# Retention and a gated projection in one Trainium2 kernel: sums asked for with the scores, batch 1's transposes in other banks and sooner, the first stage reordered

## The chip, the cores and the metric

The kernel runs on one core of one Trainium2 chip. The metric is the device time of one execution in microseconds (us). The core's engines are named here as in the profile: PE (TensorE, matrix multiplication), DVE (VectorE), ACT (ScalarE), POOL (GpSimd) and SP (SyncE, which issues the DMAs).

## The reference

Eight batches of eight heads, 576 positions and 64 channels per head. Retention is attention with a decay by distance in place of a softmax; its output is the input of a feed-forward part with a SiLU gate.

```python
scale = 1.0 / np.sqrt(D_)
scores = scale * np.matmul(q, k.transpose(0, 1, 3, 2))
gamma = 1.0 - 2.0 ** (-5.0 - np.arange(H, dtype=np.float32))
rel = pos[:, None] - pos[None, :]
Dmat = np.where(rel >= 0, gamma[:, None, None] ** rel[None, :, :], 0.0)
ret = scores * Dmat[None, :, :, :]
attn = np.matmul(ret, v)                       # (8, 8, 576, 64)
x = attn.transpose(0, 2, 1, 3).reshape(4608, 512)
h = x @ w_in                                   # 512 -> 2048
g = h * (1.0 / (1.0 + np.exp(-beta * h)))
out = g @ w_out                                # 2048 -> 512
```

## The kernel before

**Retention in chunks.** The decay is split into a factor for each query row (`gq`) and one for each key row (`gv`, put on v). A batch's first 512 positions are four chunks of 128; the last 64 positions of all batches are gathered into four tail chunks that form a ninth block. Within a chunk the kernel takes scores, masks them on DVE (`R`) and multiplies by v. Earlier chunks come in through a state, the sum of k-transposed times v over the chunks so far, which is multiplied by q (`a_cross`, `crosses4`). The output lands already transposed in `xT`, the input of the feed-forward part.

**Batches 0 and 1.** These two go through `spans`: two spans of 256 rows, each span in two interleaved halves `r`. `pre_q`, `pre_k` and `pre_v` scale and cast q, k and v to bf16 (`qs`, `kn`, `vn`); `t_q` and `t_k` transpose on PE into a PSUM tile `T` that is copied to `qT` and `kT`; `a_sc` makes scores (one `R` for each row half of the array; a last argument of 0 or 1 masks one of the two at a time); `states` and `state_out` build the state and copy it to `sbd`; `a_O` and `a_cross` make the output `O`; `a_x` copies it to `xT`. `second(i)` does the last three for the chunks `i` and `i + 1` of batch 1. Later batches are transposed by DMA (`x_q`, `x_k`).

**Feed-forward.** `up`, `ups` and `up_spans` multiply `w_in` by `xT`, one tile of 128 of the 2,048 features (`fo`) at a time, into a PSUM tile `ph`; ACT applies SiLU. Blocks 0 to 2 then go through `down`, a plain projection with `w_out` (four row tiles `ms`, in steps of four `fo`). From block 3 (`SB`) on, the down projection is done with seven products in place of eight (`seven_a`, `seven_mm`, `seven_out`), and an odd `fo` takes a second step on DVE (L776), which multiplies by a ratio.

**Folds.** From block 2 on, the states of four eighths at a time are made beside the scores, in two PSUM banks, one of `mm` and one of `st` (`state_banks`). `fold` adds them one after the other to running sums on DVE (L585) and casts the sums to bf16. The banks are free when their sums are taken. One of the sums is held in the tile `warm`, whose zeros served the warm-up before.

**PSUM.** Eight banks: `mm` has three, `O` and `sc` two each, `st` one.

**Order.** Everything is written out by hand. The first stage (L928 to L986) is a list of calls, in the order in which each engine takes its work. Between its calls stand warm-up matmuls on zeros (`warm_up`), f32, of 256 or 128 columns; a f32 matmul is two pairs of a weight load and a matmul in the trace. Everything after is `merged`: `fill` holds PE's dense steps (up and down), numbered from 0, and `streams` hold the other steps, each with the number of the fill step ahead of which it is issued. `d0` is the number of batch 0's first down step, `u1` = `d0` + 16 that of batch 1's first up step, and the steps `d0` + 12 to `d0` + 15 are the last row tile of batch 0's down projection. From block 3 on, `t0` is the step ahead of which a block's scores are issued, and `queued` hands out the rest of that work (folds, casts, masks) at the listed steps.

Of the kernel before, what the change touches and what calls it, by code (L numbers as in the profile page):

```python
# [19 lines left out]
def kernel(  # L20
# [10 lines left out]
    nc = tc.nc  # L31
# [230 lines left out]
    for g in range(NP):  # L262
        load_w_in(g)

    def warm_up(n, cols=256, tag="mm"):
        ph = psum.tile([P, MB], F32, name="ph", tag=tag, bufs=dict(mm=3, st=1)[tag])
        for _ in range(n):
            nc.tensor.matmul(ph[:, :cols], warm[:, :P], warm[:, :cols], start=True, stop=True,
                             skip_group_check=True)

    def betas():
# [30 lines left out]
    def gains(g, c):  # L302
        return g[:, c, :].unsqueeze(2).to_broadcast([P, H, D])
# [73 lines left out]
            live.update({b * CB + 2 * u + x: {} for x in range(2)})  # L377
        copy(spans[b, u]["kn"][:, r], span_tiles[b, u, 0][:, :, r])  # L378

    def pre_v(b, u, r, multiply=nc.gpsimd.tensor_tensor):  # L380

        vn = spans[b, u]["vn"][r] = sb.tile([P, H, D], BF16, name="vn", tag="vn", bufs=7)
        multiply(vn[:], span_tiles[b, u, 1][:, :, r], gains(gv, 2 * u + r), ALU.mult)
# [23 lines left out]

    def t_k(b, u, r):
        late_span = b and u
        T = psum.tile([P, HP, P], BF16, name="T", tag="sc" if late_span else "mm" if b + u + r == 0 else "O",  # L410
                      bufs=3 if b + u + r == 0 else 2)
        for p in range(HP):
            nc.tensor.transpose(T[:, p, :], heads(spans[b, u]["kn"][:, r], p), ident[:])  # L413
        (nc.vector.tensor_copy if late_span or b == 0 and u != r else nc.scalar.copy)(spans[b, u]["kT"][:, r], T[:])
# [346 lines left out]
    def up(m, fo, c0=0, cn=CB):  # L761
        if m not in gts:
            gts[m] = sb.tile([P, FO, CB, P], BF16, name="gT", tag="gT", bufs=1)
        w = slice(c0 * PC, (c0 + cn) * PC)
        ph = psum.tile([P, CB, P], F32, name="ph", tag="mm", bufs=3)
        ph = ph.rearrange("f i s -> f (i s)")[:, :cn * P].rearrange("f (i s) -> f i s", i=CB)
        ns = 2 if m == SB and fo in halved else 1
        for ko in range(KO):
            for n in range(ns):
                cs = slice(n * CB // ns, (n + 1) * CB // ns)  # L770
                nc.tensor.matmul(ph[:, cs], w_in_sb[:, ko, fo * P:(fo + 1) * P], xts[m][:, ko, cs, w],  # L771
                                 start=(ko == 0 and n == 0), stop=(ko == KO - 1), skip_group_check=ns > 1)
        if m >= SB and fo % 2:
            h = scratch[0][:, fo // 2 % 4].rearrange("f (i s) -> f i s", i=CB)
            nc.scalar.activation(h, ph, ACT.Silu, scale=beta_sb[:, fo:fo + 1])  # L775
            nc.vector.tensor_scalar(gts[m][:, fo], h, ratio[:, fo // 2:fo // 2 + 1], None, ALU.mult)  # L776
            return
        nc.scalar.activation(gts[m][:, fo, :, w], ph, ACT.Silu, scale=beta_sb[:, fo:fo + 1])  # L778
# [146 lines left out]

    warm_up(1)  # L928
    betas()
    betas_safe()  # L930
    warm_up(3)
    for n in range(2):
        pre_q(0, n)
    pre_k(0, 0, 1, nc.vector.tensor_copy)
# [3 lines left out]
    t_k(0, 0, 0)  # L938
    for n in range(2, 4):
        pre_q(0, n)  # L940
    warm_up(1, 128)
    a_sc(0, 0, 0, 0)
    warm_up(1, 128)
    t_q(0, 1, slice(0, 2), nc.scalar.copy)
    t_q(0, 1, slice(2, CB), nc.vector.tensor_copy)
    a_sc(0, 0, 0, 1)
    pre_k(0, 1, 0)
    pre_k(0, 1, 1, nc.scalar.copy)
    warm_up(1, 128)
    t_k(0, 1, 0)  # L950
    t_k(0, 1, 1)
    pre_v(0, 0, 0)
    a_sc(0, 0, 1, 0)
    pre_v(0, 0, 1, nc.vector.tensor_tensor)
    a_sc(0, 0, 1, 1)
    a_sc(0, 1, 0)
    warm_up(2, 128, "st")
    states(0, 0)
    a_sc(0, 1, 1)
    states(0, 1)  # L960
    state_out(0, 0)
    state_out(0, 1)
    for r in range(2):
        pre_v(0, 1, r)
    for c in range(2):
        new_O(c)
    a_O(0, 0, 0)
    a_O(0, 0, 1, last=False)
    a_x(0)
    a_cross(1, False)  # L970
# [52 lines left out]
    def second(i):  # L1023
# [3 lines left out]
        if i > CB:  # L1027
# [12 lines left out]
               [(d0 + 7, F(pre_q, 1, n)) for n in range(4)] + [(d0 + 12.5, F(pre_q, XB, n)) for n in range(4)] + [(d0 + 11.6, F(t_q, 1, 0)), (d0 + 12.6, F(t_q, 1, 1))],  # L1040
               [(d0 + 8, F(pre_k, 1, 0, r)) for r in range(2)] + [(d0 + 9, F(pre_v, 1, 0, r)) for r in range(2)] +
               [(d0 + 12.6, F(t_k, 1, 0, 0)), (d0 + 12.6, F(t_k, 1, 0, 1)), (d0 + 14, F(a_sc, 1, 0, 0)), (d0 + 14, F(a_sc, 1, 0, 1)),
                (d0 + 14, F(states, 1, 0)), (d0 + 14, F(state_out, 1, 0)), (d0 + 14, F(state_out, 1, 1)), (d0 + 15.9, F(second, 4))],
# [71 lines left out]
    for n in range(1, B):  # L1115

        take = [i for i in todo if seq[i][0] == n + 1 or n == B - 1]
        todo = todo[len(take):]
        b, t = n + 1, base[n]
        t0 = t + lead.get(n, 0)  # L1120
        if n == 1:
            at = [t + 17, base[b] - 8.3]
        elif n < SB:
            at = [t + 3, t + 18]
        else:
            at = [t0 - 13, t0 + 2] if n < B - 1 else [t0 - 9.5, t0 - 2.5]
        for i, x in zip(take, at, strict=True):
            streams.append(pair_prep(i, x))
        if n == 1:
            streams.append([(d0 + 6.1, F(mask, late, [1, CB], [CB, PC // 2])),  # L1130
                            (d0 + 6.2, F(mask, tri, [1, TL]))])
            streams.append([(at[0], F(group1, b, (0,))), (at[1], F(group1, b, (1,))), (at[1] + 4.1, F(both4, b))])
        elif n < SB:
            streams.append([(t + 16, F(first_states, b))] * (b == XB + 1) +
                           [(t + 19, F(group1, b, (0, 1))), (t + 25.9, F(both4, b))])
        elif n == B - 1:
            outs = []
            streams.append([(t0, F(tail_scores, take[0])), (t + 13, F(both_tails, take[0], outs))] +
                           queued([t + 16.3, t + 17.6, t + 20.5, t + 22.5], outs))
# [41 lines left out]
```

## Time and profile before

| | |
|---|---|
| time, median of 3 runs | 290.85 us (290.37 to 290.99) |
| profiled execution: time, span | 290.9 us, 289.2 us |
| PE busy | 281.4 us, 97% of the span |
| DVE, ACT, POOL busy | 185.3, 169.7, 134.7 us |
| granted PE clock | 1.00 |
| data moved by DMA | 54.05 MB, 187 GB/s on average |

The span runs from the first to the last instruction; the time of the execution has 1.7 us more. All times inside the span are counted from its start. PE's matmuls overlap, and their ends are modelled, so the time that PE loses at a wait is read from one start to the next.

### The profile page before, as it was taken

How to read it: one execution, taken by the hardware profiler on the slowest of the kernel's cores; microseconds unless marked ns; L12 is line 12 of the kernel's file. 1: busy time of each engine (PE TensorE's matmuls, PEld its weight loads, DVE VectorE, ACT ScalarE, POOL GpSimd, SP SyncE). 2: the span in 40 equal slices, each digit the busy share in tenths (PEclk: the TensorE clock that was granted, in tenths of full speed). 3: DMA queues.
4: the chain of work that ended last, by engine and by line, in shares of the span. 5: the costliest groups of instructions: out<-in, count | busy, mean ns of one | idle time of the engine just before them, and what ended most of it. 6: DMA issues, size and time to landing. Idle time of an engine off the chain costs nothing.

```text
span 289.2 us, 8713 instructions
## 1 busy us (share of the span) xinstructions
PE 281.4 (97%) x3643; PEld 178.1 (62%) x3643; DVE 185.3 (64%) x343; ACT 169.7 (59%) x295; POOL 134.7 (47%) x258
## 2 busy tenths in 40 slices
PE   6899999999999999999999999999999999999995
PEld 4564446874454445568854884578557845884584
DVE  5983545714798287289759865995598455642673
ACT  4367727586968892775358615771576156827730
POOL 6366019933993874197587466634089300000000
PEclk9999999999999999999999999999999999999999
DMA  6999999977999999989899999990689330002004
GB/s 216 305 363 385 382 307 294 175 161 195 194 174 277 248 156 207 291 204 168 189 260 246 169 258 247 186 148 0 211 178 163 74 147 3 2 37 108 2 4 141
DMA packets 120567, 54.05 MB, mean 187 GB/s; under 512 B 93888, under 2 KB 113360, under 8 KB 120528
## 3 DMA queue, kind: packets, MB, share of 16 engines
q1 hardware_dynamic: 120496, 53.49, 79.6%
q8 instruction: 28, 0.46, 0.7%
q14 instruction: 11, 0.09, 0.1%
q10 hardware_dynamic: 32, 0.01, 0.0%
HBM read 36.71 MB, written 9.44 MB: 160 GB/s over the span
## 4 chain that ended last, share of the span: by engine, by line
PE 93%; DMA 3%; DVE 1%; issue 1%; SPq 1%; ACT 0%; POOL 0%; ACTq 0%
PE ph L771 39%; PE po L896 15%; PE U L808 11%; PE Z L808 7%; PE W L808 7%; PE O L549 4%; PE ph L863 4%; DMA kvn<-in_k_dram 3%; PE sc L549 2%; PE st L549 2%; PE ph L878 1%; PE O L476 1%; PE st L509 1%; PE T L413 0%; DVE gT L776 0%
## 5 line engine op out<-in xcount | busy, mean ns | idle before, releaser
L771 PE MATMUL ph<-xT,w_in_sb 128*128 128x512 bf16 (+1 forms) x576 | 116.3, 358 | 0.4 <-DVE sum L585 0.2
L771 PEld LDWEIGHTS <-w_in_sb 128*128 128x128 bf16 x576 | 55.0, 98 | 54.4 <-DVE sum L585 0.9
L778 ACT ACTIVATE gT<-ph,beta_sb 128x512 bf16<-128x512 f32 (+1 forms) x92 | 58.2, 641 | 39.5 <-PE ph L771 38.6
L808 PEld LDWEIGHTS <-sa 128*128 128x128 bf16 x480 | 46.8, 98 | 5.6 <-DVE sa L792 0.2
L776 DVE TENSOR_SCALAR gT<-hs,ratio 128x512 bf16<-128x512 f32 x48 | 25.6, 532 | 35.8 <-ACT hs L775 35.5
L329 POOL TENSOR_TENSOR qs<-qn,gq 128x256 bf16<-128x256 f32 x48 | 30.1, 659 | 31.4 <-DMA qn<-in_q_dram 21.7
L775 ACT ACTIVATE hs<-ph,beta_sb 128x512 f32<-128x512 f32 x48 | 33.0, 688 | 19.5 <-PE ph L771 18.8
L792 DVE TENSOR_TENSOR sa<-gT 128x1024 bf16<-128x1024 bf16 (+1 forms) x54 | 42.9, 834 | 1.4 <-PE Z L808 1.2
L896 PE MATMUL po<-w_out_sb,gT 128*128 128x512 bf16 x192 | 43.3, 379 | 0.0
L311 POOL TENSOR_TENSOR vn<-kvn,gv 128x256 bf16<-128x256 f32 x48 | 35.2, 757 | 2.2 <-DMA kvn<-in_v_dram 1.7
L366 POOL CAST kn<-kvn 128x128 bf16<-128x128 f32 (+1 forms) x72 | 26.9, 412 | 15.3 <-DMA kvn<-in_k_dram 15.3
L896 PEld LDWEIGHTS <-gT 128*128 128x128 bf16 x192 | 18.1, 98 | 20.8
L808 PE MATMUL Z<-b,sa 128*128 128x256 bf16 x192 | 23.0, 273 | 0.0
L808 PE MATMUL U<-b,sa 128*128 128x256 bf16 x192 | 22.9, 273 | 0.0
L292 DVE TENSOR_TENSOR R<-sc,late 128x512 bf16<-128x512 f32 x24 | 15.4, 679 | 11.3 <-issue 10.0
L808 PEld LDWEIGHTS <-gT 128*128 128x128 bf16 x192 | 18.7, 98 | 3.2
L254 DVE TENSOR_TENSOR b<-wt 128x512 bf16<-128x512 f32 x20 | 16.4, 878 | 1.8 <-ACT wt L237 1.7
L682 ACT CAST xT<-O 128x512 bf16<-128x512 f32 x19 | 9.8, 599 | 5.7 <-PE O L549 5.7
L378 POOL CAST kn<-kvn 128x512 bf16<-128x512 f32 x6 | 3.8, 656 | 16.5 <-DMA kvn<-in_k_dram 16.5
L808 PE MATMUL W<-b,gT 128*128 128x256 bf16 x96 | 11.5, 273 | 0.0
L808 PE MATMUL U<-b,gT 128*128 128x256 bf16 x96 | 11.5, 272 | 0.0
L808 PE MATMUL W<-b,sa 128*128 128x256 bf16 x96 | 11.5, 272 | 0.0
(120 smaller groups left out, 314.7 us busy)
## 6 DMA issues: line engine op xcount, KB each, us to landing
qn<-in_q_dram SPq DMA_DIRECT2D x16, 512.0 KB, 5.4
out_dram<-ot SPq DMA_DIRECT2D x32, 256.0 KB, 3.2
wt<-in_moe_w_out_dram SPq DMA_DIRECT2D x8, 512.0 KB, 9.2
kvn<-in_k_dram SPq DMA_DIRECT2D x12, 256.0 KB, 5.6
kvn<-in_v_dram SPq DMA_DIRECT2D x12, 256.0 KB, 6.7
kvn<-in_k_dram SPq DMA_DIRECT2D x24, 128.0 KB, 4.6
kvn<-in_v_dram SPq DMA_DIRECT2D x24, 128.0 KB, 4.1
wt<-in_moe_w_in_dram SPq DMA_DIRECT2D x5, 512.0 KB, 9.4
```

Of the source, the lines that this page charges most:

```text
L254: nc.vector.tensor_tensor(to, x, y, op)
L311: nc.gpsimd.tensor_tensor(vn[:, hs], v[:, hs], g[:, hs], ALU.mult)
L329: nc.gpsimd.tensor_tensor(batch[b]["qs"][:, cs, to], q_tiles[b][:, hs, cs].rearrange("p h i d -> p i h d"), gq[:, cs, hs].unsqueeze(3).to_ ...
L366: nc.gpsimd.tensor_copy(kn[:, c % 2, to], t[:, 0, hs])
L549: ins = nc.tensor.matmul(out, lhsT, rhs, start=start, stop=stop, skip_group_check=True)
L771: nc.tensor.matmul(ph[:, cs], w_in_sb[:, ko, fo * P:(fo + 1) * P], xts[m][:, ko, cs, w], start=(ko == 0 and n == 0), stop=(ko == KO - 1), ...
L775: nc.scalar.activation(h, ph, ACT.Silu, scale=beta_sb[:, fo:fo + 1])
L776: nc.vector.tensor_scalar(gts[m][:, fo], h, ratio[:, fo // 2:fo // 2 + 1], None, ALU.mult)
L778: nc.scalar.activation(gts[m][:, fo, :, w], ph, ACT.Silu, scale=beta_sb[:, fo:fo + 1])
L792: nc.vector.tensor_tensor(sums_a[0][:, held_in[j], ks], quarter(m, *x, ks), quarter(m, *y, ks), op)
L808: nc.tensor.matmul(chains[c, n][:, 0 if alone else p], a, sevens[k // 2][:, j - 1, k % 2, :], start=j in (3, 4, 1) and k == 0 and (alone o ...
L896: nc.tensor.matmul(po[:, :nn], gT[:, fo, ms, :], w_out_sb[:, fo, n0:n0 + nn], start=(fo == 0), stop=(fo == FO - 1))
```

## The change

Four things change.

1. Warm-up. The f32 warm-ups ahead of the first transposes have 512 columns instead of 256 (`warm_long`, one and two instead of one and three). The short ones between the later calls are bf16 with 512 columns (`warm_short`, five calls). In the trace's count that is 22 weight loads and matmuls instead of 36.
2. First stage. Batch 0's second `kn` of the second span goes from ACT to POOL. The scores of span 0's second heads half are issued between the two `t_k` of span 1 instead of behind both. `t_k(0,1,0)` is copied by ACT instead of DVE. Of `vn(0,0,1)`, DVE makes the lower four heads and ACT the upper four, with one activation for each head (DVE made all of it); of `vn(0,1,1)`, POOL makes the lower and DVE the upper half (POOL made all). The products `a_O(0,0,0)` and the second span's `pre_v` are issued ahead of `a_sc(0,1,1)` and `states(0,1)`.
3. Batch 1's first span. Its transposes of k go to the banks `st` and `mm` instead of `O`, the copy of `t_k(1,0,1)` to DVE instead of ACT, and `t_q(1,0)` is copied in two halves by ACT and DVE instead of in one by ACT. `t_q(1,1)`, `t_k`, the scores, the states and `second(4)` are asked for 0.4 to 1.4 steps sooner. Three up tiles of batch 1 (`fo` 10 to 12) are done in two halves of 256 columns.
4. Folds. In blocks 3 to 6 the first fold is asked for at `t0`, right behind the scores, instead of at `t0 + 0.1`, which is one fill step later.

```diff
-    def warm_up(n, cols=256, tag="mm"):
+    def warm_short(n, tag="mm"):
         ph = psum.tile([P, MB], F32, name="ph", tag=tag, bufs=dict(mm=3, st=1)[tag])
+        zeros = warm[:].bitcast(BF16)
         for _ in range(n):
-            nc.tensor.matmul(ph[:, :cols], warm[:, :P], warm[:, :cols], start=True, stop=True,
+            nc.tensor.matmul(ph[:], zeros[:, :P], zeros, start=True, stop=True, skip_group_check=True)
+
+    def warm_long(n):
+        ph = psum.tile([P, 2, 256], F32, name="ph", tag="mm", bufs=3)
+        for _ in range(n):
+            nc.tensor.matmul(ph[:], warm[:, :P], warm[:].unsqueeze(1).to_broadcast([P, 2, 256]), start=True, stop=True,
                              skip_group_check=True)
...
-    def pre_v(b, u, r, multiply=nc.gpsimd.tensor_tensor):
-
-        vn = spans[b, u]["vn"][r] = sb.tile([P, H, D], BF16, name="vn", tag="vn", bufs=7)
-        multiply(vn[:], span_tiles[b, u, 1][:, :, r], gains(gv, 2 * u + r), ALU.mult)
+    def pre_v(b, u, r, multiply=nc.gpsimd.tensor_tensor, hs=slice(0, H)):
+
+        if spans[b, u]["vn"][r] is None:
+            spans[b, u]["vn"][r] = sb.tile([P, H, D], BF16, name="vn", tag="vn", bufs=7)
+        vn, v = spans[b, u]["vn"][r], span_tiles[b, u, 1]
+        if multiply is None:
+            for h in range(hs.start, hs.stop):
+                nc.scalar.activation(vn[:, h], v[:, h, r], ACT.Copy, scale=gv[:, 2 * u + r, h:h + 1])
+            return
+        multiply(vn[:, hs], v[:, hs, r], gains(gv, 2 * u + r)[:, hs], ALU.mult)
...
-        T = psum.tile([P, HP, P], BF16, name="T", tag="sc" if late_span else "mm" if b + u + r == 0 else "O",
-                      bufs=3 if b + u + r == 0 else 2)
+        tag = "sc" if late_span else "st" if b and r == 0 else "mm" if b or u + r == 0 else "O"
+        T = psum.tile([P, HP, P], BF16, name="T", tag=tag, bufs=dict(mm=3, sc=2, O=2, st=1)[tag])
...
-        (nc.vector.tensor_copy if late_span or b == 0 and u != r else nc.scalar.copy)(spans[b, u]["kT"][:, r], T[:])
+        (nc.vector.tensor_copy if late_span or u < r else nc.scalar.copy)(spans[b, u]["kT"][:, r], T[:])
...
-        ns = 2 if m == SB and fo in halved else 1
+        ns = 2 if m == SB and fo in halved or m == 1 and 10 <= fo < 13 else 1
...
-    warm_up(1)
+    warm_long(1)
     betas()
     betas_safe()
-    warm_up(3)
+    warm_long(2)
...
-    warm_up(1, 128)
+    warm_short(1)
     a_sc(0, 0, 0, 0)
-    warm_up(1, 128)
+    warm_short(1)
...
     a_sc(0, 0, 0, 1)
     pre_k(0, 1, 0)
-    pre_k(0, 1, 1, nc.scalar.copy)
-    warm_up(1, 128)
+    pre_k(0, 1, 1)
+    low, high = slice(0, HP), slice(HP, H)
+    warm_short(2)
     t_k(0, 1, 0)
+    a_sc(0, 0, 1, 0)
     t_k(0, 1, 1)
     pre_v(0, 0, 0)
-    a_sc(0, 0, 1, 0)
-    pre_v(0, 0, 1, nc.vector.tensor_tensor)
     a_sc(0, 0, 1, 1)
+    pre_v(0, 0, 1, None, high)
+    pre_v(0, 0, 1, nc.vector.tensor_tensor, low)
     a_sc(0, 1, 0)
-    warm_up(2, 128, "st")
+    warm_short(1, "st")
     states(0, 0)
+    pre_v(0, 1, 0)
+    pre_v(0, 1, 1, hs=low)
+    pre_v(0, 1, 1, nc.vector.tensor_tensor, high)
+    for c in range(2):
+        new_O(c)
+    a_O(0, 0, 0)
     a_sc(0, 1, 1)
     states(0, 1)
     state_out(0, 0)
     state_out(0, 1)
-    for r in range(2):
-        pre_v(0, 1, r)
-    for c in range(2):
-        new_O(c)
-    a_O(0, 0, 0)
     a_O(0, 0, 1, last=False)
...
-  (d0 + 11.6, F(t_q, 1, 0)), (d0 + 12.6, F(t_q, 1, 1))
+  (d0 + 11.6, F(t_q, 1, 0, slice(0, 2))), (d0 + 11.6, F(t_q, 1, 0, slice(2, CB), nc.vector.tensor_copy)), (d0 + 11.6, F(t_q, 1, 1))
...
-  (d0 + 12.6, F(t_k, 1, 0, 0)), (d0 + 12.6, F(t_k, 1, 0, 1)), (d0 + 14, F(a_sc, 1, 0, 0)), (d0 + 14, F(a_sc, 1, 0, 1)),
-  (d0 + 14, F(states, 1, 0)), (d0 + 14, F(state_out, 1, 0)), (d0 + 14, F(state_out, 1, 1)), (d0 + 15.9, F(second, 4))
+  (d0 + 11.6, F(t_k, 1, 0, 0)), (d0 + 11.6, F(t_k, 1, 0, 1)), (d0 + 12.6, F(a_sc, 1, 0, 0)), (d0 + 12.6, F(a_sc, 1, 0, 1)),
+  (d0 + 13.6, F(states, 1, 0)), (d0 + 13.6, F(state_out, 1, 0)), (d0 + 13.6, F(state_out, 1, 1)), (d0 + 15, F(second, 4))
...
-  queued([t0 + 0.1, t0 + 0.9, t0 + 1.7, t0 + 2.6, ...] if n == SB else [t0 + 0.1, t0 + 0.9, t0 + 0.9, t0 + 1.8, t0 + 2.6] + ...)
+  queued([t0, t0 + 0.9, t0 + 1.7, t0 + 2.6, ...] if n == SB else [t0, t0 + 0.9, t0 + 0.9, t0 + 1.8, t0 + 2.6] + ...)
```

More of the change, by code (lines that the diff above doesn't have):

```diff
@@ L1039 @@
                 (base[2] - 4.5, F(release, 4))],
-               [(d0 + 7, F(pre_q, 1, n)) for n in range(4)] + [(d0 + 12.5, F(pre_q, XB, n)) for n in range(4)] + [(d0 + 11.6, F(t_q, 1, 0)), (d0 + 12.6, F(t_q, 1, 1))],
+               [(d0 + 7, F(pre_q, 1, n)) for n in range(4)] + [(d0 + 12.5, F(pre_q, XB, n)) for n in range(4)] + [(d0 + 11.6, F(t_q, 1, 0, slice(0, 2))), (d0 + 11.6, F(t_q, 1, 0, slice(2, CB), nc.vector.tensor_copy)), (d0 + 11.6, F(t_q, 1, 1))],
                [(d0 + 8, F(pre_k, 1, 0, r)) for r in range(2)] + [(d0 + 9, F(pre_v, 1, 0, r)) for r in range(2)] +
-               [(d0 + 12.6, F(t_k, 1, 0, 0)), (d0 + 12.6, F(t_k, 1, 0, 1)), (d0 + 14, F(a_sc, 1, 0, 0)), (d0 + 14, F(a_sc, 1, 0, 1)),
-                (d0 + 14, F(states, 1, 0)), (d0 + 14, F(state_out, 1, 0)), (d0 + 14, F(state_out, 1, 1)), (d0 + 15.9, F(second, 4))],
+               [(d0 + 11.6, F(t_k, 1, 0, 0)), (d0 + 11.6, F(t_k, 1, 0, 1)), (d0 + 12.6, F(a_sc, 1, 0, 0)), (d0 + 12.6, F(a_sc, 1, 0, 1)),
+                (d0 + 13.6, F(states, 1, 0)), (d0 + 13.6, F(state_out, 1, 0)), (d0 + 13.6, F(state_out, 1, 1)), (d0 + 15, F(second, 4))],
                [(d0 + 10, F(pre_k, 1, 1, r)) for r in range(2)] + [(d0 + 12, F(pre_v, 1, 1, r)) for r in range(2)] +
@@ L1144 @@
                 streams.append([(t - 4, F(first_states, b))])
-            streams.append([(t0, F(scores, b, (0, 1), rest))] + queued([t0 + 0.1, t0 + 0.9, t0 + 1.7, t0 + 2.6, t0 + 3.4, t0 + 4.2, t0 + 4.3, t0 + 5.1, t0 + 6] if n == SB else
-                           [t0 + 0.1, t0 + 0.9, t0 + 0.9, t0 + 1.8, t0 + 2.6] + span(t0 + 3.4, 4, 0.9), rest))
+            streams.append([(t0, F(scores, b, (0, 1), rest))] + queued([t0, t0 + 0.9, t0 + 1.7, t0 + 2.6, t0 + 3.4, t0 + 4.2, t0 + 4.3, t0 + 5.1, t0 + 6] if n == SB else
+                           [t0, t0 + 0.9, t0 + 0.9, t0 + 1.8, t0 + 2.6] + span(t0 + 3.4, 4, 0.9), rest))
             by = t + 17.4 if n == SB else t + 14.5 if n == SB + 1 else t + 12.8
```

## The prediction

> **What bounds the kernel now.** I read the page first, then the busy time by stretch, then what TensorE (PE) waited for, and last the order in time around each wait.
>
> ```profile
> span 289.2 us, 8713 instructions
> ...
> PE 281.4 (97%) x3643; PEld 178.1 (62%) x3643; DVE 185.3 (64%) x343; ACT 169.7 (59%) x295; POOL 134.7 (47%) x258
> ...
> PE 93%; DMA 3%; DVE 1%; issue 1%; SPq 1%; ACT 0%; POOL 0%; ACTq 0%
> ```
>
> PE is busy for 281.4 of 289.2 us and carries 93% of the chain that ended last. Only 7.8 us of the span are not PE's. The stretches (PE, PEld, DVE, ACT, POOL, then granted clock, DMA share, GB/s) say where they lie:
>
> ```profile
> 0.00:5.00 5.00, 2.39 (x5) 1.52 (x6) 2.25 (x15) 2.63 (x4) 3.72 (x25) 1.00 0.52 169
> 5.00:10.00 5.00, 4.53 (x49) 3.39 (x48) 4.25 (x8) 1.24 (x3) 1.86 (x3) 1.00 1.13 308
> 10.00:15.00 5.00, 4.14 (x78) 2.94 (x76) 4.71 (x9) 2.41 (x5) 2.76 (x4) 1.00 1.14 314
> ...
> 120.00:289.20 169.20, 165.51 (x2203) 112.97 (x2201) 112.45 (x196) 90.60 (x149) 66.59 (x116) 1.00 0.64 140
> ```
>
> Half of the idle time (3.9 us) is in the first 15 us, where inputs land, and most of the 3.7 us in the last row is the store after PE's end. The list of PE's waits has five lines of the first stage and these two:
>
> ```profile
> PE ph L771 <- DVE sum L585: 0.2, 1, 0.2
> PE ph L771 <- DVE xT L495: 0.2, 1, 0.2
> ```
>
> So three places can pay: the first stage, the wait for `xT` and the wait for `sum`. What PE gains there should reach the end one for one, since nothing else holds it afterwards.
>
> **Sums asked for with the scores.** In four blocks the first fold moves from behind the next up-projection tile to ahead of it. Where that tile is an odd one (three of the four), the fold on DVE now stands ahead of its multiplication (L776).
>
> ```profile
> 175.02 0.45 PE L549 MATMUL st<-vn,kn 64*64 64x64 bf16 x32
> ...
> 177.20 1.26 DVE L776 TENSOR_SCALAR gT<-hs,ratio 128x512 bf16<-128x512 f32 x1 [2.83 <-ACT hs L775]
> 178.38 0.41 DVE L585 TENSOR_TENSOR warm<-sum,st 128x256 f32<-128x256 f32 x1
> 178.82 0.42 DVE L585 TENSOR_TENSOR sum<-warm,st 128x256 f32<-128x256 f32 x1
> ...
> 178.51 0.59 PE L771 MATMUL ph<-xT,w_in_sb 128*128 128x512 bf16 x2
> 179.30 0.39 PE L771 MATMUL ph<-xT,w_in_sb 128*128 128x512 bf16 x1 [0.20 <-DVE sum L585]
> ```
> ```profile
> 24.13 1.73 PE ph L771 x8
> ```
>
> The states end at 175.47, DVE idles 2.83 us for ScalarE's `hs`, multiplies for 1.26 us, and only then sums; PE wants the sums' bank. With the fold first, both sums take 0.41 + 0.42 us from 175.5 and the bank is free by 176.4, 2.5 us before PE needs it; the multiplication still waits for `hs`, so nothing is pushed back. A matmul of this form starts 1.73 / 8 = 0.216 us after the one before. The two at 178.51 should have been followed at 178.94, and the next came at 179.30: the gain is 0.36 us. (The wait's 0.20 counts only from the modelled end of the matmul before.) The other blocks show no such wait, so they gain nothing.
>
> **Batch 1's transposes.** None of the moved steps issues a DMA or POOL work. `t_q(1,1)`, both `t_k(1,0,r)`, the scores and `second(4)` each move one step of the down projection earlier (the states stay ahead of step `d0` + 14); the `T` of `t_k` go to the banks `st` and `mm`.
>
> ```profile
> 49.99 0.39 PE L413 MATMUL T<-ident,kn 128*128 128x128 bf16 x4
> 50.56 0.28 PE L771 MATMUL ph<-xT,w_in_sb 128*128 128x256 bf16 x1 [0.18 <-DVE xT L495]
> ...
> 46.13 0.68 PE L549 MATMUL sc<-qT,kT 64*64 64x128 bf16 x32
> ...
> 49.18 0.64 PE L549 MATMUL O<-R,vn 64*64 64x128 bf16 x32
> ...
> 46.62 2.48 DVE L447 TENSOR_TENSOR R<-sc,causal 128x512 bf16<-128x512 f32 x4 [1.01 <-PE sc L549]
> ...
> 41.94 1.17 POOL L378 CAST kn<-kvn 128x512 bf16<-128x512 f32 x2 [13.09 <-DMA kvn<-in_k_dram]
> 43.59 2.05 POOL L383 TENSOR_TENSOR vn<-kvn,gv 128x512 bf16<-128x512 f32 x2 [0.48 <-DMA kvn<-in_v_dram]
> ```
> ```profile
> 42.97 0.61 PE L405 MATMUL T<-ident,qs 128*128 128x128 bf16 x8
> ```
> ```profile
> 14.44 0.41 PE sc L549 x15
> ...
> 44.89 0.45 PE T L413 x8
> 45.33 0.86 PE po L896 x4
> ```
>
> Today `second(4)` is followed only by four transposes (0.22 us by the chain's 0.45 for eight) before the up projection wants `xT`: from 49.99 they would end at 50.21, and the projection starts at 50.56, so 0.35 us are lost. Moved up, a step of 0.86 us lies between, longer than what is missing, and the wait goes whole. The inputs allow it: `kn` is cast by 43.11, and its transposes would start about 43.9 (`t_q` at 42.97, two groups of 0.45); `vn` ends at 45.64, the states would start about 46.6 (45.2, scores 0.5, a step 0.86); two steps and the states still lie between scores and `second(4)`, as today (46.13 to 49.18, with R's end at 49.10), so that slack of 0.1 us is kept. What is late next is the copy of the last `T`: DVE must copy half of `qT`, the rest of `qT` and `kT` before the scores at about 45.2, and ends about 45.1. I take 0.33 us, from 0 to 0.35. The split of three up tiles into halves adds 12 matmuls; a half costs half, so I charge 0.03 us.
>
> **The first stage.** It holds the terms I know least.
>
> ```profile
> 1.25 1.22 PE L268 MATMUL ph<-warm 128*128 128x256 f32 x2 [1.25 <-DVE warm L135]
> ...
> 4.01 2.93 PE L268 MATMUL ph<-warm 128*128 128x256 f32 x6
> 6.73 0.73 PE L405 MATMUL T<-ident,qs 128*128 128x128 bf16 x8
> 7.39 0.86 PE L413 MATMUL T<-ident,kn 128*128 128x128 bf16 x8
> ...
> 13.84 0.38 PE L509 MATMUL st<-vn,kn 64*128 64x128 bf16 x4 [0.17 <-DVE vn L383]
> ...
> 14.79 0.62 PE L509 MATMUL st<-vn,kn 128*128 128x128 bf16 x8
> ...
> 17.95 2.08 PE L878 MATMUL ph<-xT,w_in_sb 128*128 128x256 bf16 x16
> ```
> ```profile
> 3.90 0.25 ACT L156 ACTIVATE gv<-lg 128x72 f32<-128x72 f32 x1
> ...
> 11.64 0.59 ACT L414 COPY kT<-T 128x512 bf16<-128x512 bf16 x1 [0.51 <-PE T L413]
> ```
> ```profile
> 10.60 0.68 DVE L447 TENSOR_TENSOR R<-sc,causal 128x512 bf16<-128x512 f32 x1
> 11.42 0.42 DVE L414 COPY kT<-T 128x512 bf16<-128x512 bf16 x1
> ...
> 12.60 1.19 DVE L383 TENSOR_TENSOR vn<-kvn,gv 128x512 bf16<-128x512 f32 x1
> ```
> ```profile
> L227 ACT ACTIVATE w_out_sb<-wt,rbeta_sb x3: 721/733/735, 33.8 to 37.0; 128x512 bf16<-128x512 f32 x3
> ```
>
> Warm-ups first. Six instructions of 256 columns took 2.93 us and two took 1.22, so one costs 1.71 / 4 = 0.43. The new second group has four of 512 columns, 4 x 0.85 = 3.4 us where 2.6 stood, and would end at 7.6. But the eight transposes from 6.73 to 7.39 took 0.66 us where eight later took 0.45: PE doubled its rate there, at about 7.0, with the granted clock at 1.00 throughout. So the last warm-up ends at about 7.3 and the transposes come 0.55 us late. DVE copies `qT` 0.4 us late and ends its early work (R to 11.28 today) at about 11.7. That costs nothing: DVE then copied `kT(0,1,0)` to 11.84, which ScalarE does now, and the next scores, moved ahead of `t_k(0,1,1)`, are there by then. Their two R (2.48 / 4 = 0.62 each) run from about 11.75 to 13.0. If that cover were gone, the 0.4 would reach the stage's end.
>
> The last input of `states(0,0)` decides: today DVE's `vn`, ending at 13.79 with PE at 13.84. Afterwards DVE does half of it (0.6 us, to 13.6) and ScalarE the other half, in four activations behind two copies of `kT`. Today's started at 11.64; POOL now casts both `kn` one after the other (1.17 / 2 = 0.59), so the second copy starts some 0.4 later and ends about 12.65. POOL gives half a `vn` away for that cast, so `w_in`'s casts behind it come no later. Four by the 72-column row (0.25) make at most 1.0 us, so 13.65, or 13.4 if they overlap; I take 13.6, since a row of 72 columns is nearest to 64, and PE at 13.62. The far bound is L227's 0.73 for 512 columns: 2.9 us, to 15.6.
> By the Trainium skill, page "ScalarE: Activation LUTs", section "Rules for kernel authors", an activation costs about 0.3 us plus 0.83 ns an element, so 0.35 for 64 by estimate, 1.4 for four, PE at 14.1 and a first stage 0.3 us slower than before, the sum 290.5; the trace's 0.25 for 72 columns is below that rule, and I go by the row.
>
> PE then does the four states (0.3, as eight take 0.62), half of the outputs (half of 0.57, and 0.1 for the switch) and the scores, which no longer wait for R (0.35, as from 14.44 to 14.79 in the chain), so `states(0,1)` starts at about 14.65 where it started at 14.79. Behind it ScalarE's `sbd`, `xT`, `sbd` keep their order, and PE has 0.3 us of outputs less to do. I take 0.2 us for the stage, from 0.45 gained (vn already whole at 13.35) to 1.8 lost (at 15.6, the far bound): what `vn` is later than 13.8 is lost.
>
> **The sum.** 0.36 + 0.33 + 0.20 - 0.03 = 0.86 us off the profiled execution's 290.9 us (1.7 of it outside the span): 290.04. The runs shown have the median 290.85, from 290.37 to 290.99, so the profiled one is typical, and I forecast 290.0 us, 0.3% less. About 0.2% (0.58 us) is what a measurement of this kernel can tell from no change: the line is at 290.27.
>
> **The rivals.** *The first stage gives nothing, or loses up to 0.4 us.* Its mechanism is ScalarE's queue: activations of 0.35 us (a fifth of the way from the 0.25 row to L227's 0.73) make `vn` whole at 14.05. DVE's work, late by the warm-ups, would do the same. Against it speaks the row nearest in size. It gives 290.2 to 290.6, mostly within 0.2%. Chance 0.22. (The Trainium skill's 0.35, cited above, is this rival.)
> *A new wait eats batch 1's gain.* The scores would wait for DVE's third copy, or `second(4)` for R, whose slack is 0.1 us. It costs the 0.33 and perhaps as much again: 290.4 to 290.7. Chance 0.10.
> *The rate doubles sooner.* The first warm-ups are twice as long, PE idles less before 7 us, and its rate might rise by 4 us: the second group would then end at 5.8, the transposes wait for `qs` alone, and the stage gains perhaps 0.2 more: 289.8. For it: the rate rose 3 us after PE became steadily busy at 4.01. Against: PE still idles between the two groups, from 3.1 on (1.25 + 0.16 + 1.71). Chance 0.08.
> By the Trainium skill, "TensorE: Matmul & The Clock Gate", Part 1, the gate opens after a busy window of about 3.4 us whose phase is free-running; the trace's rise at 7.0 fits that, and no run here shows the phase.
> *Slower.* The four activations on ScalarE cost near 0.7 us each (a small operation priced like L227). `vn` is whole at 15.6, PE's states, outputs and everything behind are held, and 1.8 us lost less the 0.66 gained elsewhere give 292.0. From 0.45 us each (`vn` at 14.46) nothing is left of the gain, and from 0.6 the kernel is slower by 0.2%. The 0.25 row speaks against it. Chance 0.08.
>
> **How the numbers follow.** The forecast keeps 0.52. Faster by over 0.2%: 0.47 of the forecast, 0.08 of the sooner rate, 0.10 of the first two rivals' better ends, 0.65. Slower by over 0.2%: the last rival and 0.01 for two mishaps at once, 0.09. The rest, 0.26, is within 0.2%. The range runs from 289.4 (the stage's best bound gives 289.8, and the runs' lowest lies 0.48 under their median) to 290.8 (the two middle rivals' upper ends, and 0.1 of that spread) and leaves out the slow rival and the far tails.
>
> **What would show it.** PE's waits no longer list `sum` or `xT`; DVE's two sums follow the states at once; the up projection of batch 1 follows its transposes without a gap. In the first stage `T` from `qs` starts near 7.3, four activations of about 0.2 us stand on ScalarE, `states(0,1)` starts near 14.65 and the first up projection near 17.75 instead of 17.95. I am wrong if that last number is above 17.95, or if a wait of PE appears between 43 and 51 us.

## The result, and the profile after

The changed kernel takes 289.92 us (median of 22 runs, 288.93 to 291.1), the kernel before 290.62 us beside it (22 runs, 290.12 to 291.63). The ratio of the two sets of runs is 0.997, 95% interval 0.9961 to 0.998: by it 0.87 us less, from 0.58 to 1.13; the medians alone lie 0.70 apart. Forecast were 290.0 us and a gain of 0.86. The profiled execution took 289.33 us, 1.6 us less than the profiled one of before. The runs scatter, and that pair shows more than the change, so its terms have to be read one by one.

The page, with span, busy time and chain:

```profile
span 287.6 us, 8701 instructions
...
PE 278.9 (97%) x3618; PEld 177.2 (62%) x3648; DVE 185.3 (64%) x345; ACT 169.7 (59%) x298; POOL 132.3 (46%) x259
...
PE 94%; DMA 3%; issue 1%; SPq 1%; ACT 0%; POOL 0%; DVE 0%; ACTq 0%
```

PE still carries the chain. It has 30 records fewer than PEld, where before both had 3643: 30 matmuls are missing from this trace, so PE's 278.9 us can't be set against the 281.4 of before, and a wait of one matmul (0.2 us) with the releaser "issue" is a missing record. PE's waits:

```profile
PE sc L561 <- ACT kT L426: 0.8, 2, 0.5
PE po L908 <- issue: 0.8, 5, 0.2
...
PE T L425 <- DVE kn L384: 0.4, 1, 0.4
PE st L521 <- ACT sbd L540: 0.2, 1, 0.2
```

`sum` and `xT` are gone from the list, as forecast. New is `sbd`: the third `states` waits until ACT has copied the second out of the only bank `st`. The first stage on PE in order of time:

```profile
1.25 2.07 PE L274 MATMUL ph<-warm 128*128 128x512 f32 x2 [1.25 <-DVE warm L135]
...
6.15 0.61 PE L417 MATMUL T<-ident,qs 128*128 128x128 bf16 x8
...
10.67 0.40 PE L425 MATMUL T<-ident,kn 128*128 128x128 bf16 x4 [0.54 <-POOL kn L384]
...
12.42 0.31 PE L561 MATMUL sc<-qT,kT 64*64 64x128 bf16 x8 [0.37 <-ACT kT L426]
12.66 0.39 PE L269 MATMUL ph<-warm 128*128 128x512 bf16 x1
12.98 0.66 PE L521 MATMUL st<-vn,kn 64*128 64x128 bf16 x8
...
14.15 0.62 PE L521 MATMUL st<-vn,kn 128*128 128x128 bf16 x8
...
15.62 0.62 PE L521 MATMUL st<-vn,kn 64*128 64x128 bf16 x8 [0.17 <-ACT sbd L540]
...
17.31 2.15 PE L890 MATMUL ph<-xT,w_in_sb 128*128 128x256 bf16 x16
```

ACT's and DVE's share of `vn`, and POOL's two casts with what they waited for:

```profile
12.26 1.06 ACT L393 ACTIVATE vn<-kvn,gv 128x64 bf16<-128x64 f32 x4
```
```profile
12.66 0.55 DVE L395 TENSOR_TENSOR vn<-kvn,gv 128x256 bf16<-128x256 f32 x1
```
```profile
10.00 1.17 POOL L384 CAST kn<-kvn 128x512 bf16<-128x512 f32 x2 [2.47 <-DMA kvn<-in_k_dram]
```

`states(0,1)` starts at 14.15 (before 14.79) and the first up projection at 17.31 (before 17.95), 0.64 us sooner. Only half of that is the change. POOL's cast of the second span's k, which waits for a transfer, began at 10.31 in the trace of before:

```profile
10.31 0.62 POOL L378 CAST kn<-kvn 128x512 bf16<-128x512 f32 x1 [2.51 <-DMA kvn<-in_k_dram]
```

From that cast to the first up projection it is 7.64 us before (17.95 - 10.31) and 7.31 after: 0.33 us are the change, 0.31 an earlier landing. Batch 1:

```profile
42.40 1.06 PE L417 MATMUL T<-ident,qs 128*128 128x128 bf16 x16
...
44.69 0.64 PE L561 MATMUL sc<-qT,kT 64*64 64x128 bf16 x32
45.49 0.81 PE L908 MATMUL po<-w_out_sb,gT 128*128 128x512 bf16 x3 [0.16 <-issue]
46.23 0.81 PE L561 MATMUL st<-vn,kn 64*64 64x64 bf16 x32
...
49.62 0.39 PE L425 MATMUL T<-ident,kn 128*128 128x128 bf16 x4
49.84 0.60 PE L783 MATMUL ph<-xT,w_in_sb 128*128 128x256 bf16 x4
```

The up projection now follows its transposes at once (49.62 to 49.84). But the whole stretch from the first `T` of `qs` to it went from 7.59 us (42.97 to 50.56) to 7.44: 0.15 us, not the 0.35 of the wait. The folds, on DVE and PE, after and then before:

```profile
174.44 0.42 DVE L597 TENSOR_TENSOR warm<-sum,st 128x256 f32<-128x256 f32 x1 [1.16 <-PE st L561]
174.89 0.42 DVE L597 TENSOR_TENSOR sum<-warm,st 128x256 f32<-128x256 f32 x1
```
```profile
204.81 3.40 PE L783 MATMUL ph<-xT,w_in_sb 128*128 128x512 bf16 x15
```
```profile
204.69 3.48 PE L771 MATMUL ph<-xT,w_in_sb 128*128 128x512 bf16 x15
```

The sums follow the states at once. And the same fifteen matmuls, in a block where the list of waits shows nothing, take 3.40 us instead of 3.48: waits below the list's display went too.

### The profile page after: what moved, and what is told of

It is laid out like the page before. It is cut to its first block, busy times and chain, and to the rows that moved or that the text cites. A ratio compares the mean times of both kernels' runs of the same rounds, so it can differ in the third digit from the quotient of the medians.

```text
span 287.6 us, 8701 instructions
## 1 busy us (share of the span) xinstructions
PE 278.9 (97%) x3618; PEld 177.2 (62%) x3648; DVE 185.3 (64%) x345; ACT 169.7 (59%) x298; POOL 132.3 (46%) x259
## 4 chain that ended last, share of the span: by engine, by line
PE 94%; DMA 3%; issue 1%; SPq 1%; ACT 0%; POOL 0%; DVE 0%; ACTq 0%
PE ph L783 39%; PE po L908 14%; PE U L820 11%; PE Z L820 7%; PE W L820 7%; PE O L561 4%; PE ph L875 4%; DMA kvn<-in_k_dram 3%; PE sc L561 2%; PE st L561 2%; PE st L521 1%; PE ph L890 1%; PE T L425 1%; PE O L488 1%; SPq L86 0%
## 5 line engine op out<-in xcount | busy, mean ns | idle before, releaser
L783 PE MATMUL ph<-xT,w_in_sb 128*128 128x512 bf16 (+1 forms) x570 | 114.2, 354 | 0.9
L783 PEld LDWEIGHTS <-w_in_sb 128*128 128x128 bf16 x588 | 56.4, 98 | 52.1 <-DVE xT L694 0.2
L788 DVE TENSOR_SCALAR gT<-hs,ratio 128x512 bf16<-128x512 f32 x48 | 27.1, 565 | 31.2 <-ACT hs L787 30.7
L908 PE MATMUL po<-w_out_sb,gT 128*128 128x512 bf16 x183 | 42.0, 379 | 1.0 <-issue 0.8
L804 DVE TENSOR_TENSOR sa<-gT 128x1024 bf16<-128x1024 bf16 (+1 forms) x54 | 41.6, 812 | 0.8 <-PE Z L820 0.6
L317 POOL TENSOR_TENSOR vn<-kvn,gv 128x256 bf16<-128x256 f32 x48 | 33.2, 715 | 3.0 <-issue 2.0
L372 POOL CAST kn<-kvn 128x128 bf16<-128x128 f32 (+1 forms) x72 | 25.1, 386 | 14.8 <-DMA kvn<-in_k_dram 14.7
L254 DVE TENSOR_TENSOR b<-wt 128x512 bf16<-128x512 f32 x20 | 15.6, 840 | 1.9 <-ACT wt L237 1.8
L384 POOL CAST kn<-kvn 128x512 bf16<-128x512 f32 x7 | 4.4, 647 | 16.0 <-DMA kvn<-in_k_dram 16.0
```

What stands on the lines that cost most here:

```text
L254: nc.vector.tensor_tensor(to, x, y, op)
L317: nc.gpsimd.tensor_tensor(vn[:, hs], v[:, hs], g[:, hs], ALU.mult)
L372: nc.gpsimd.tensor_copy(kn[:, c % 2, to], t[:, 0, hs])
L804: nc.vector.tensor_tensor(sums_a[0][:, held_in[j], ks], quarter(m, *x, ks), quarter(m, *y, ks), op)
L908: nc.tensor.matmul(po[:, :nn], gT[:, fo, ms, :], w_out_sb[:, fo, n0:n0 + nn], start=(fo == 0), stop=(fo == FO - 1))
```

## The experiments

**Each part alone.** Four kernels carry one part each on the kernel before. The three halved tiles are in none of them.

```diff
folds_only
-  queued([t0 + 0.1, ...] if n == SB else [t0 + 0.1, ...])
+  queued([t0, ...] if n == SB else [t0, ...])
batch1_only
+  T of t_k(1,0,r) in the banks st and mm, t_k(1,0,1) copied by DVE, t_q(1,0) by both
-  (d0 + 12.6, F(t_q, 1, 1)), ... (d0 + 14, F(a_sc, 1, 0, 0)), ... (d0 + 14, F(states, 1, 0)), ... (d0 + 15.9, F(second, 4))
+  (d0 + 11.6, F(t_q, 1, 1)), ... (d0 + 12.6, F(a_sc, 1, 0, 0)), ... (d0 + 13.6, F(states, 1, 0)), ... (d0 + 15, F(second, 4))
stage_only
+  the new order of the calls and the shares of vn and kn; warm_up(1), (3), (1, 128)... as before
warm_only
-  warm_up(1) ... warm_up(3) ... warm_up(1, 128) x3 ... warm_up(2, 128, "st")
+  warm_long(1) ... warm_long(2) ... warm_short(1) x2, (2) ... warm_short(1, "st")
```

> The kernel before with the folds' change alone. The forecast's reckoning: PE's wait for the sum (0.36 us from start to start at 179 us) goes, 290.6 - 0.36, ratio 0.9988; DVE's first sum starts within 0.1 us of the end of the states. Rival (the first stage is the whole gain): the profile's wait of 0.2 us comes back elsewhere and the time is that of before, ratio 1.000.

> The kernel before with batch 1's change alone (banks, copies and times of its transposes, scores and second(4); no halved tiles). The forecast's reckoning: the wait for xT goes and PE's first up matmul of batch 1 follows its transposes at once, 0.33 us gained, ratio 0.9989. Rival, from the profile after the change (0.15 to 0.2 us between the two anchors): half of it is lost again among the moved steps, ratio 0.9994. Rival: a wait in the moved steps eats all of it, 1.000.

> The kernel before with the first stage's new order and distribution alone, under the old warm-up matmuls. The forecast's reckoning: vn whole near 13.4 to 13.6 us and the first up projection 0.2 us sooner than in a run of the kernel before with the same landings, ratio 0.9993; the transposes of q start at 6.7 as before. Rival (the warm-ups carry the first stage's gain): ratio 1.000, first up projection near 17.9 less whatever the landings are early.

> The kernel before with the new warm-up matmuls alone. The forecast's reckoning: the second group of warm-ups holds PE to about 7.3, the transposes of q start late, and without the new order nothing covers it: 0.0 to 0.4 us slower, ratio 1.000 to 1.0014. Rival (the rate of PE doubles sooner because PE idles less before 4 us): the transposes of q start at 6.1 to 6.7, ratio 0.999 to 1.000.

Against the kernel before (290.92 us, 35 runs): folds 0.9985 (0.9975 to 0.9995), batch 1 0.9991 (0.9979 to 1.0002), stage 0.9985 (0.9974 to 0.9995), warm-ups 1.0005 (0.9992 to 1.0017). The product is 0.9966, inside the interval of the whole. But a time is unsure by 0.3 us and more, as large as the parts themselves, and the intervals of batch 1 and the warm-ups hold 1. The terms have to be read from the traces.

*Folds.* The 0.36 us wait of the trace of before is in no other trace with the old folds. In batch1_only, whose folds are those of before, DVE's multiplication took 0.49 us where that one trace had 1.26, and the sums were ready in time:

```profile
177.27 0.49 DVE L776 TENSOR_SCALAR gT<-hs,ratio 128x512 bf16<-128x512 f32 x1 [2.83 <-ACT hs L775]
177.67 0.41 DVE L585 TENSOR_TENSOR warm<-sum,st 128x256 f32<-128x256 f32 x1
```

So the 0.36 is there in some executions only. What is always there is small: at about 124, 177 and 206 us, the up tile behind the scores starts 0.075 to 0.077 us late in each of the five traces taken with the old folds, and in none with the new ones. That PE there waits for ACT, which has to read one of only two free banks `mm`, is how I read it; no run tested that reason. Three such waits make 0.23 us in every execution. The measured 0.44 us (0.15 to 0.73) is wide enough to hold that and part of the 0.36.

*Batch 1.* Its stretch is 7.44 us here as in the changed kernel, and again in the five traces below that leave batch 1's part as it is in the changed kernel. In the five traces with the old batch 1 it is 7.59 to 7.60: 0.15 us more, whatever the first stage does.

*Warm-ups.* Alone they give nothing, and their rate was half for longer:

```profile
7.51 0.97 PE L417 MATMUL T<-ident,qs 128*128 128x128 bf16 x8
```

The transposes from `qs` started 0.78 us later than before (6.73) and 1.36 later than in the changed kernel (6.15). Yet its stretch from the cast of k to the up projection is 7.64 us, that of before. What PE does ahead of about 10 us was hidden here.

*Stage.* The new order alone has 7.58 us. PE's end of it:

```profile
13.11 0.71 PE L268 MATMUL ph<-warm 128*128 128x128 f32 x4
13.76 0.62 PE L527 MATMUL st<-vn,kn 64*128 64x128 bf16 x8
...
18.04 0.71 PE L896 MATMUL ph<-xT,w_in_sb 128*128 128x256 bf16 x5
```

`vn` is no longer what `states(0,0)` starts behind; the old f32 warm-up is, four instructions and 0.65 us. In the changed kernel the bf16 one is over in 0.32 (12.66 to 12.98). So the stage's gain should come from the order and that single warm-up together. The time of stage_only, 0.44 us less (0.15 to 0.76), is more than its stretch's 0.06 explains; where the rest comes from stays open.

**The single warm-up, the share of `vn`, no warm-ups, no halves.** Three take something out of the changed kernel; stage_one_short is stage_only with the last warm-up changed alone.

```diff
stage_one_short (on stage_only)
-    warm_up(2, 128, "st")
+    warm_short(1, "st")
vn_on_dve (on the changed kernel)
-    pre_v(0, 0, 1, None, high)
-    pre_v(0, 0, 1, nc.vector.tensor_tensor, low)
+    pre_v(0, 0, 1, nc.vector.tensor_tensor)
no_warm_ups (on the changed kernel)
-    warm_long(1) ... warm_long(2) ... warm_short(1) ... warm_short(1) ... warm_short(2) ... warm_short(1, "st")
no_halved_tiles (on the changed kernel)
-    ns = 2 if m == SB and fo in halved or m == 1 and 10 <= fo < 13 else 1
+    ns = 2 if m == SB and fo in halved else 1
```

> The first stage's new order alone, as in the run before, but with the last warm-up (the two f32 matmuls ahead of states(0,0)) replaced by the one bf16 matmul of the change. Theory (with vn earlier, that warm-up itself is what states(0,0) waits behind): from the first cast of k's second span to the first up projection 7.3 us, as after the change, where the order alone took 7.58 and the kernel before 7.64. Rival (the longer first warm-ups and the sooner rise of PE's rate made the difference): 7.55 to 7.64.

> The changed kernel with vn(0,0,1) made whole by DVE again, no activations on ScalarE. Theory (the halves make vn whole sooner, DVE would take 1.19 us from about 2.65 us after k's second span's cast): states(0,0) ends 0.4 to 0.5 us later, and from the cast to the first up projection it takes 7.7 to 7.8 us instead of 7.31. Rival (ScalarE's bank of the states decides later anyway): 7.3 to 7.4.

> The changed kernel without any warm-up matmul. Theory (the first stage hangs on the landing of k's second span, and PE's rate matters little behind it): from that cast to the first up projection 7.2 to 7.5 us, time within 0.1% of the changed kernel, ratio to before 0.996 to 0.998. Rival (the warm-ups are what lets PE run at its full rate behind 10 us): PE's spacing of 128 columns stays 0.107 us beyond 11 us, the stage takes 7.8 us or more, ratio 0.999 to 1.003.

> The changed kernel with the three up tiles of batch 1 (fo 10 to 12) whole again. Theory (12 matmuls more cost 0.0025 us each): from batch 1's first up matmul to the 60th activation of ScalarE 0.03 us less than after the change, so 67.4 us. Rival (the halves hide a wait): a wait of PE of 0.1 us or more appears between 60 and 64 us.

stage_one_short, one execution of 291.03 us, in which k landed late:

```profile
11.10 1.17 POOL L390 CAST kn<-kvn 128x512 bf16<-128x512 f32 x2 [3.73 <-DMA kvn<-in_k_dram]
```
```profile
13.51 0.31 PE L567 MATMUL sc<-qT,kT 64*64 64x128 bf16 x8 [0.37 <-ACT kT L432]
14.08 0.66 PE L527 MATMUL st<-vn,kn 64*128 64x128 bf16 x8 [0.26 <-POOL vn L401]
...
18.41 0.27 PE L896 MATMUL ph<-xT,w_in_sb 128*128 128x256 bf16 x1
```

The 0.26 at 14.08 is no wait: the warm-up's own record is missing there, and from the scores to the states it is 0.57 us, as in the changed kernel (12.42 to 12.98). The stretch is 7.31 us, all of the changed kernel's gain. One warm-up of the eight is worth 0.27 us under the new order, and the others nothing against those they replaced. A still shorter one would bring little more: in the changed kernel the states start at 12.98, 0.05 us behind the end of POOL's `vn` of the first half (12.93), and their second four at 13.27, 0.06 behind the end of DVE's share (12.66 + 0.55).

vn_on_dve took 292.82 us for a reason that I had not asked about. By stretch (PE, PEld, DVE, ACT, POOL, granted clock, DMA share, GB/s):

```profile
9.00:10.00 1.00, 0.23 (x1) 0.00 (x0) 0.50 (x1) 0.00 (x0) 0.00 (x0) 1.00 1.17 295
10.00:11.00 1.00, 0.55 (x7) 0.39 (x8) 1.00 (x3) 0.32 (x1) 0.00 (x0) 1.00 1.06 259
11.00:12.00 1.00, 0.47 (x6) 0.19 (x6) 1.00 (x3) 0.26 (x1) 0.68 (x2) 1.00 1.10 310
12.00:13.00 1.00, 1.00 (x22) 0.71 (x23) 0.32 (x1) 0.57 (x1) 0.49 (x1) 0.62 0.93 239
...
19.00:20.00 1.00, 1.00 (x16) 0.68 (x14) 0.78 (x2) 0.71 (x2) 0.50 (x2) 0.96 1.03 321
```

`qs` and k came late, PE was busy for 1.25 of the three microseconds from 9 to 12, and the granted clock fell to 0.50. (In after_again, below, PE was busy for 1.50 of the same three, and the clock stayed at 1.00; how much idling brings the fall is not shown.) A second at 0.62 holds 0.24 us of full speed, one at 0.96 lacks 0.08: the fall lasted from 12.24 to 19.08 us. The stretch grew to 9.49 us. The Trainium skill, "TensorE: Matmul & The Clock Gate", Part 1, gives the clock gate a window of 3413 ns; two of them are 6.83 us, near the 6.84 here, but no run shows where a window begins. The run says nothing of `vn`, so the kernel was run again (below).

no_warm_ups is slower than before by 2.1 us, 1.0073 (1.005 to 1.0097). PE stays at half rate through the whole stage, and eight matmuls of 128 columns reach full rate only at 18.46:

```profile
16.51 1.04 PE L521 MATMUL st<-vn,kn 128*128 128x128 bf16 x8
...
18.46 0.62 PE L521 MATMUL st<-vn,kn 64*128 64x128 bf16 x8
```

Its stretch is 9.03 us, 1.72 more than with them. Warm-ups are needed; which ones stand ahead of 10 us hardly matters.

no_halved_tiles took 290.45 us in one execution. From batch 1's first up matmul to ACT's sixty-first activation of an up tile, far behind the three tiles, it is 67.37 us with whole tiles and 67.46 with halves, and this stretch scatters from 67.26 to 67.81 among the other kernels. The two traces differ by 0.09 us, less than that scatter, so what the halves cost or bring is not settled.

**Scores and states together again.** In batch 1 the wait went, and 0.2 us of it was given back. In the trace of before, scores and states stand together (46.13, 46.63, and the down projection again at 47.35):

```profile
46.63 0.79 PE L549 MATMUL st<-vn,kn 64*64 64x64 bf16 x32
```

Afterwards each has a step of the down projection of its own around it. A matmul of the down projection is followed by the next in 0.216 us, and by a transpose on the whole array just as fast, but by scores or states on a quarter of the array (64*64 in the profile) in 0.309; and scores followed by the down projection take 0.57 where scores followed by states took 0.50. If that is the price of one more switch to such small matmuls and back, `states` asked for with the scores should bring it back. split_copy also has half of the second `sbd` copied by DVE, against the new wait for `st`.

```diff
after_again: the changed kernel, once more
states_beside (on the changed kernel)
-    (d0 + 13.6, F(states, 1, 0)), (d0 + 13.6, F(state_out, 1, 0)), (d0 + 13.6, F(state_out, 1, 1))
+    (d0 + 12.6, F(states, 1, 0)), (d0 + 12.6, F(state_out, 1, 0)), (d0 + 12.6, F(state_out, 1, 1))
states_beside_split_copy (on states_beside)
-    e = nc.vector.tensor_copy if b and c > 1 else nc.scalar.copy
+    e = nc.vector.tensor_copy if b and c > 1 or not b and c == 1 and j else nc.scalar.copy
-    a_sc(0, 1, 1)
+    a_sc(0, 1, 1, 2)
+    a_sc(0, 1, 1, 3)
vn_on_dve_2: vn_on_dve, once more
```

> The changed kernel once more, beside the next ones. Theory: ratio to before 0.997, from the first cast of k's second span to the first up projection 7.31 us, wherever that cast lies, and no small waits of 0.076 us behind the three blocks' scores. Rival (the stage's gain came from early landings in the one profile): that stretch is 7.5 us or more.

> The changed kernel with batch 1's states(1,0) issued right behind its scores again, ahead of the same down step, instead of one down step later. Theory (each switch between the down projection and small matmuls costs PE 0.09 to 0.1 us, and the change made two of them more): from the first transpose of t_q to batch 1's first up matmul 0.19 us less, 7.25 instead of 7.44 us. Rival (the switches were not the loss; vn or the bank of the states makes PE wait): 7.4 us or more. The time moves by 0.06%, less than the rounds can tell.

> As the run before, and in the first stage the copy of the states of span 0 (chunk 1) shared: ScalarE copies one half, DVE the other, ahead of the last two R. Theory (states(0,2) waits 0.24 us for ScalarE's second copy out of the same bank): that wait goes, and from the cast of k's second span to the first up projection 7.1 instead of 7.31 us, ratio to the changed kernel 0.9985 with the run before's gain. Rival (DVE's R, late by the copy, or its xT becomes the last): 7.25 to 7.35.

> The changed kernel with vn(0,0,1) whole on DVE, run again, since in the look before PE fell back to half its rate near 12.9 us and hid the effect. Theory: with PE at its full rate, 7.7 to 7.8 us from the cast of k's second span to the first up projection instead of 7.31. Rival: 7.3 to 7.4, the halves bring nothing. Either way the fall back to half rate, if it returns, shows as a spacing of 0.107 us for 128 columns.

Against the kernel before (290.83 us, 32 runs): after_again 0.9979 (0.9966 to 0.9992), states_beside 0.9971 (0.9961 to 0.9981), states_beside_split_copy 0.9979 (0.9969 to 0.999), vn_on_dve_2 0.9972 (0.9962 to 0.9981). The intervals overlap: no version is shown to beat the changed kernel, and a quarter of a microsecond is below what these times tell apart. The traces tell more. states_beside:

```profile
4.03 3.78 PE L274 MATMUL ph<-warm 128*128 128x512 f32 x4
7.61 1.03 PE L417 MATMUL T<-ident,qs 128*128 128x128 bf16 x8
...
45.53 0.64 PE L561 MATMUL sc<-qT,kT 64*64 64x128 bf16 x32
46.00 0.79 PE L561 MATMUL st<-vn,kn 64*64 64x64 bf16 x32
...
50.45 0.60 PE L783 MATMUL ph<-xT,w_in_sb 128*128 128x256 bf16 x4
```

From the first `T` of `qs` at 43.24 it is 7.21 us, 0.23 less than the 7.44 of all seven traces with the states apart, and no wait of PE is listed there: the price of the further switch is shown. Its first stage took 7.77 us, though. The rows of betas came late, the four warm-ups at half rate ended at 7.6, and k landed at 10.43: DVE was late with the second span's `qs`, and PE still had `T` from `qs` and warm-ups to do when `kn` was there. POOL's first cast also took 0.94 us instead of 0.61, so `kn` was there at 11.37, but PE was busy with the rest until 11.62. This is the case that the prediction named, the cover gone, and it cost 0.46 us over 7.31 (by this one trace).

In split_copy the copy on DVE held up DVE's masks, and `states` waited all the same, now for DVE; the stretch was 7.60 us:

```profile
15.69 0.62 PE L529 MATMUL st<-vn,kn 64*128 64x128 bf16 x8 [0.24 <-DVE sbd L548]
...
45.35 1.09 PE L569 MATMUL st<-vn,kn 64*64 64x64 bf16 x32
```

Nor did batch 1's gain come back whole: 7.51 us. PE was 0.65 us earlier there than in states_beside (45.35 for 46.00), while POOL finished `vn` at 45.70, so the states took 1.09 instead of 0.79 us. Scores and states can stand together only where `vn` is whole by then.

vn_on_dve_2 kept the full clock. DVE's whole `vn` and what PE does behind it:

```profile
13.48 0.81 DVE L395 TENSOR_TENSOR vn<-kvn,gv 128x512 bf16<-128x512 f32 x1
```
```profile
14.34 0.38 PE L521 MATMUL st<-vn,kn 64*128 64x128 bf16 x4 [0.15 <-DVE vn L395]
```

The second half of `states(0,0)` waits for it; 7.57 us, so the four activations are worth 0.26 us. These 0.26 and the 0.27 of the short warm-up are not two gains to be added. PE waits for the later of `vn` and the warm-up: the new order under the old warm-up brings 0.06 (stage_only), the short warm-up under the old order nothing (warm_only), both together 0.33. after_again has them all, with the latest landing of the study:

```profile
11.51 1.17 POOL L384 CAST kn<-kvn 128x512 bf16<-128x512 f32 x2 [4.11 <-DMA kvn<-in_k_dram]
```
```profile
18.77 1.47 PE L890 MATMUL ph<-xT,w_in_sb 128*128 128x256 bf16 x12
```

7.26 us. All traces together, from the first cast of the second span's k to the first up projection:

| kernel | cast | up projection | between, us |
|---|---|---|---|
| before | 10.31 | 17.95 | 7.64 |
| folds_only | 10.05 | 17.69 | 7.64 |
| warm_only | 10.71 | 18.35 | 7.64 |
| batch1_only | 11.13 | 18.74 | 7.61 |
| stage_only | 10.46 | 18.04 | 7.58 |
| vn_on_dve_2 | 10.81 | 18.38 | 7.57 |
| stage_one_short | 11.10 | 18.41 | 7.31 |
| no_halved_tiles | 10.79 | 18.10 | 7.31 |
| changed kernel | 10.00 | 17.31 | 7.31 |
| after_again | 11.51 | 18.77 | 7.26 |
| states_beside_split_copy | 10.01 | 17.61 | 7.60 |
| states_beside | 10.43 | 18.20 | 7.77 |
| no_warm_ups | 11.12 | 20.15 | 9.03 |
| vn_on_dve | 11.32 | 20.81 | 9.49 |

The old order has one value within 0.03 us, whatever the landing, the warm-ups or the moment at which PE's rate doubled (between 5 and 10 us, another in each trace). So the stage runs from that landing, which moves by 1.5 us from execution to execution.

## Why the prediction was right, and where it was not

The total came out at 0.87 for 0.86 us by the ratio, 0.70 by the medians. By the traces the terms are 0.33 (stage), 0.15 (batch 1) and 0.23 (folds), 0.71 together, and up to 0.36 more where the sum wait occurs: 0.7 to 1.1, with the halves unsettled. Each of the three gains was off in size, and the errors offset each other: that the total fits to 0.01 us is luck.

- *Folds, 0.36 forecast.* The mechanism held: the sums follow the states and the wait is gone. The size was wrong both ways. The step that failed was to take one profiled execution's wait as a fixed one: it hung on a multiplication of 1.26 us, which took 0.49 in the four other traces with the old folds. And "the other blocks show no such wait, so they gain nothing" failed: three waits of 0.076 us were too short for the list.
- *Batch 1, 0.33 forecast, 0.15 measured.* The wait went whole, its cover, copies and casts were in time, and neither scores nor `second(4)` waited, so the second rival fell. What failed was the step that let the states move ahead of another step at no cost: the sum had no term for one more switch between dense matmuls and small ones on a quarter of the array, 0.23 us by states_beside, where `vn` is in time.
- *Stage, 0.20 forecast, 0.33 measured.* That `vn` decides held in the changed kernel: PE goes on behind it 3.27 us after the cast (13.27 for 10.00), and 3.31 was forecast (13.62 for 10.31). The term that was mis-sized is PE's work from there to `states(0,1)`: 0.3 for states, 0.38 for half the outputs and 0.35 for scores make 1.03 us, and 0.88 was measured (13.27 to 14.15), the outputs alone 0.25 (13.57 to 13.82). Behind `states(0,1)` 0.06 were forecast and nothing came: it is 3.16 us to the up projection before and after, now with the wait for `sbd` in it.
  What the forecast did not see is the last warm-up. With the old one PE would have stood behind that, not behind `vn`, and the stage would have gained 0.06 (stage_only); the shorter one carries the other 0.27, for which the forecast had no term.
  Two more readings failed, without consequence in the profile. "The transposes come 0.55 us late" was wrong there (6.15, not 7.3) and right in warm_only, and gave nothing either way; the sooner rate, a rival, occurred and brought nothing. In states_beside the delay did reach the end. The activations take 0.34 us, not the 0.25 of my nearest row, but they start 0.24 apart, so four take 1.06, near the 1.0 that I took, and the first rival, which added up four whole ones, fell. The Trainium skill, page "ScalarE: Activation LUTs", was nearer for one (0.35 by the estimate from its section "Rules for kernel authors"). The same page of the Trainium skill, section "What ACT_TABLE_LOAD costs", says that activations back to back overlap by about 93 ns; the trace agrees (0.34 - 0.24).
- *Slower.* The four activations were nowhere near 0.7 us; that rival fell.
- *What would show it.* No wait for `sum` or `xT`, sums at once, no gap in batch 1: as said. `states(0,1)` at 14.15 for 14.65 and the up projection at 17.31 for 17.75: 0.31 us of each is the landing, which the forecast held still.

## What to carry to other kernels

When two things hold an engine and end close together, removing one shows next to nothing: the share of `vn` and the short warm-up had to come together. A wait that is seen in one profile can be an accident of that execution, and one that is always there can be too short for the list: compare the same group of matmuls in several traces before a gain is booked. Where a stage begins with a transfer, measure from its landing, not from the span's start. And a block of small matmuls on a quarter of the array that is moved away from its neighbour pays for a further switch on PE, which here ate most of the wait that the move removed.

## What the runs showed of the hardware

- The landing of the same second load of k varied from 10.00 to 11.51 us over the fourteen profiled executions with the same loads ahead of it; why was not tested.
- PE's rate doubled anywhere between 5 and 10 us under nearly the same warm-ups, at about 18.5 us without any, and the granted clock fell to 0.50 for 6.84 us after three microseconds in which PE was busy for 0.23, 0.55 and 0.47 us. In after_again 0.27, 0.40 and 0.83 brought no fall. The half rate ahead of the first doubling stands at 1.00 in the granted clock; only the later fall shows there.
- A dense matmul of 512 columns ahead of one on a quarter of the array (64*64) held PE 0.309 us; ahead of another dense one or of a transpose on the whole array it was 0.216.
